# Output rows as 12 products of 128 rows in one accumulator bank, one score task moved among them, and early VectorE work moved to GpSimd and ScalarE

## The chip, the cores and the metric

The kernel runs on one core of a Trainium2 chip. The metric is the time of one execution on the device, in microseconds (us); lower is better. Engines: TensorE does matmuls (PE in the profile, PEld for its weight loads), VectorE (DVE) and ScalarE (ACT) work on tiles element by element and are the two that empty the accumulators (PSUM banks), GpSimd (POOL) works on tiles in SBUF, and SyncE (SP) issues most DMAs. Each engine takes its instructions strictly in program order, so an instruction that waits holds everything behind it on its engine.

## The reference

Two attentions over the same input of 2048 rows and 512 columns, 32 heads of 16 columns each, mixed row by row by a gate:

```python
x = A_x
g = _sigmoid((x * gate_w).sum(-1, keepdims=True))
a = _A_ref(x, A_wq, A_wk, A_wv, A_wo, A_beta)   # 4 segments of 512 rows
b = _B_ref(x, B_wqkv, B_wo)                     # all 2048 rows
return g * a + (1 - g) * b
```

A does causal softmax attention inside each segment of 512 rows, and adds a linear-attention memory that is carried from segment to segment:

```python
logits = jnp.einsum("bhqd,bhkd->bhqk", qs, ks) * scale + mask
a_dot = jnp.einsum("bhqk,bhkd->bhqd", _softmax(logits), vs)
o = g * a_mem + (1.0 - g) * a_dot
```

B is full softmax attention over the 2048 rows. Each ends in a product with its own 512 x 512 output matrix (`A_wo`, `B_wo`). All data is float32.

## The kernel before

**Units.** A prologue (to about 330 us) makes q, k, v and the memory part and stores them in DRAM. The main loop `for k in range(32)` does two units in each iteration: unit `ub = 32 + k` of B (four heads, 512 query rows against 2048 keys) and unit `ua = k` of A (four heads, one segment). There are 8 quads of heads times 4 chunks of 512 rows for either.

**Groups.** An iteration has 37 groups `n` (`NG`); `it = n // 2`. Groups 0 to 31 belong to B, 32 to 36 to A ("the A groups"). `t_group` (L620) does one: two score matmuls (L635, 64 rows each, on the two halves of the array) into two of the three banks `TB[0]`, `TB[1]`, `MB` (`T3`, taken by the longest unused first), then two exponentials on ScalarE (L641); in A groups GpSimd masks the diagonal blocks (L644, "the masks"). `pv` (L647) multiplies the exponentials with the values into the bank `PVB`, two groups behind, at most half a block at a time. Group 1 of an iteration has no `pv`, because group 0 ends the previous A unit and `fin_copy` empties `PVB`.

**Score tasks.** The softmax subtracts the maximum of each row, which is found one iteration ahead: a score task `s_b` (L565) computes 128 queries against 512 keys for two pairs of heads (L572) into one of two double banks `SBK`, used in turn by `rot("s", SBK)`, and VectorE takes the maximum (L574). The 32 tasks of unit 33 + k are laid out by hand, in `plan`: 12 in groups 20 to 31 of iteration k - 1 and 20 in groups 0 to 19 of iteration k, one in each, between the two score matmuls of the group (`between`). Six tasks `s_a` for A go into the A groups.

**Chain of maxima.** At `it == 10`, in group 21, `m_chain(k + 1)` (L578) reduces the maxima (L583) and splits them in a high and a low part: on GpSimd (L592 to L595) for chains 8 to 31, on VectorE (L597 to L599) otherwise. `m_rows` (L601) in group 24 turns the result by a matmul with the identity (L605) and writes it into the q tiles by DMA.

**End of a unit.** `fin_copy(u)` (L660) copies `PVB` to SBUF: for A units up to 30 on VectorE (L664), otherwise on ScalarE (L666). Then `fin_load` reads it back in two layouts, `fin_rec` (L678) takes the reciprocal of the sums on VectorE and multiplies it by the gates (on VectorE while `early` holds, otherwise on GpSimd), `fin_bc` spreads it by DMA into `d`, and `fin_norm` (L699, GpSimd) multiplies, in every second iteration at `it` 9 for B and 13 for A. `beside(k, it)` places these.

**Output matrices.** `load_wo(g)` (L709) at `it == 9` of iterations 1 to 4 reads 128 rows of both output matrices and splits each in a high and a low part on GpSimd (L713, L714), right behind the DMAs in program order.

**Output rows.** The first 1536 output rows are made during iterations 9 to 31, 128 rows in two iterations. `out_split` (L719) splits the operands at the end of an even iteration; then `extras` puts one job at group 1 of each iteration: `a = 0` (A's matrix) in odd iterations k, `a = 1` (B's) in the even ones that follow ("even" and "odd rows" in the text below go by the number n = k - 9 of the job, so a = 0 is an even one). A job is 12 products, three for each of four column groups (`TERMS`: high x high, high x low, low x high). In iterations 9 to 30 `out_rows` (L737) does each product as two of 64 rows, on the two halves of the array, into two banks: one of `T3` and one half of an `SBK` double bank. The score task of group 1 goes in behind the third product (`plan.pop((k, at))` with `at` 1), so `t_group` of group 1 has none. In iteration 31 `out_mm` (L723) does 12 products of 128 rows into one bank.

**Queues.** The program order of each engine is the order of these calls. The tail behind iteration 31 (L1160 on) makes the last 512 rows.

Of the kernel before, what the change touches and what calls it, by code (L numbers as in the profile page):

```python
# [7 lines left out]
FT = mybir.dt.float32  # L8
# [4 lines left out]
AF = mybir.ActivationFunctionType  # L13
OP = mybir.AluOpType
# [7 lines left out]
DM = 512  # L22
# [11 lines left out]
S_LAST = 10  # L34
# [5 lines left out]
def gated_mix_kernel(ctx, tc, xt, wq, wk, wv, wo, beta, wqkv, wob, gate_w, out):  # L40
    nc = tc.nc
    outr = out.rearrange("b s d -> (b s) d")
# [63 lines left out]
    SBK = [PS.tile([128, 2, C], FT, name=f"sbk{i}") for i in range(2)]  # L106
# [9 lines left out]
    def misc():  # L116
        return bank(mode["misc"])
# [12 lines left out]
    def rot(key, lst):  # L130
        i = cnt.get(key, 0)
        cnt[key] = i + 1
        return lst[i % len(lst)]
# [162 lines left out]
    TERMS = ((0, 0), (0, 1), (1, 0))  # L296
# [281 lines left out]
    def m_chain(k):  # L578
        mx = pair_max(k)
        if k == 1:  # L580
            nc.vector.memset(mx[:, 0], 0.0)
        if k < 32:
            nc.vector.tensor_reduce(mx[:, 1], MXB.pop(32 + k).rearrange("q j p i c -> q (j p) i c"), axis=AX.X,  # L583
                                    op=OP.max)
        else:
            nc.vector.memset(mx[:, 1], 0.0)
        del MX[k]
        mx = mx.rearrange("q u h i -> q (u h i)")
        m8 = M8[k] = W.tile([128, 2, 32], FT, name="m8")
        hi = W.tile([128, 32], HF, name="mhi")  # L590
        if 8 <= k < 32:
            nc.gpsimd.tensor_scalar(mx, mx, -1.0 / AUX, None, op0=OP.mult)  # L592
            nc.gpsimd.tensor_copy(hi, mx)
            nc.gpsimd.tensor_copy(m8[:, 0], hi)
            nc.gpsimd.tensor_tensor(m8[:, 1], mx, hi, op=OP.subtract)  # L595
        else:
            nc.vector.tensor_scalar(hi, mx, -1.0 / AUX, None, op0=OP.mult)  # L597
            nc.vector.tensor_copy(m8[:, 0], hi)
            nc.vector.scalar_tensor_tensor(m8[:, 1], mx, -1.0 / AUX, hi, op0=OP.mult, op1=OP.subtract)  # L599
# [16 lines left out]
    AT = {}  # L616
# [30 lines left out]
    def pv(u, it, lo=0, hi=None):  # L647

        kd, qd, c = UN[u]
        g, q = divmod(qd, 2)  # L650
        q0 = 128 * it if kd == "A" else 0
        hi = hi or C - q0
        last = 2 if kd == "A" else NT - 1
        vt = VA[(u // 2) % 2] if kd == "A" else VB[g % 2]
        for h in range(4):
            pt = PT[u, it, h]
            nc.tensor.matmul(PVB[32 * h:32 * h + E + 1, q0 + lo:q0 + hi], vt[:, it, 4 * q + h, :], pt[:, lo:hi],  # L657
                             start=it == 0 and lo == 0, stop=it == last and q0 + hi == C, skip_group_check=True)

    def fin_copy(u):  # L660

        ps = W.tile([128, C], FT, name="pvs", bufs=1)
        if u < 31:
            nc.vector.tensor_copy(ps, PVB)  # L664
        else:
            nc.scalar.activation(ps, PVB, AF.Copy)  # L666
        AT["pd", u] = D.tile([4, 32, C], FT, name=f"pd{u}")
        nc.sync.dma_start(AT["pd", u].rearrange("h r t -> (h r) t"), ps)
# [9 lines left out]
    def fin_rec(u):  # L678
        kd, qd, c = UN[u]
        r = AT.pop(("r", u))  # L680
        nc.vector.reciprocal(r, r)  # L681
        early = u % 32 < 7 or u in (31, 63)
        if kd == "A" and not early:
            nc.gpsimd.tensor_scalar(r, r, nq[:, qd:qd + 1], None, op0=OP.mult)
            nc.gpsimd.tensor_tensor(r, r, grow[:, 0, c], op=OP.mult)
        elif kd == "A":
            nc.vector.scalar_tensor_tensor(r, r, nq[:, qd:qd + 1], grow[:, 0, c], op0=OP.mult, op1=OP.mult)
        else:
            (nc.vector if early else nc.gpsimd).tensor_tensor(r, r, grow[:, 1, c], op=OP.mult)  # L689
        AT["rd", u] = D.tile([128, E], FT, name=f"rd{u}")  # L690
        nc.sync.dma_start(AT["rd", u], r)
# [16 lines left out]

    def load_wo(g):  # L709
        for a, w in enumerate((wo, wob)):  # L710
            raw = AT["o"][1][:, g, a]
            nc.sync.dma_start(raw, w[g * 128:(g + 1) * 128, :])
            nc.gpsimd.tensor_copy(AT["wh"][:, g, a], raw)  # L713
            nc.gpsimd.tensor_tensor(AT["wl"][:, g, a], raw, AT["wh"][:, g, a], op=OP.subtract)  # L714

# [4 lines left out]
        nc.scalar.activation(AT["oh"], o_cols(c, t), AF.Copy)  # L720
        nc.gpsimd.tensor_tensor(AT["ol"], o_cols(c, t), AT["oh"], op=OP.subtract)

    def out_mm(c, t, a):  # L723

        b = misc()
        for n, (oi, wi, g) in enumerate([(oi, wi, g) for oi, wi in TERMS for g in range(4)]):
            nc.tensor.matmul(b, (AT["oh"], AT["ol"])[oi][:, g, a], (AT["wh"], AT["wl"])[wi][:, g, a],
                             start=n == 0, stop=n == 11)
        if a == 0:
            AT["yo"] = AT["L"].tile([128, DM], FT, name="yo")  # L730
            nc.scalar.activation(AT["yo"], b, AF.Copy)
        else:
            tt = 4 * c + t
            nc.vector.tensor_tensor(AT["yo"], b, AT["yo"], op=OP.add)
            nc.sync.dma_start(outr[tt * 128:(tt + 1) * 128, :], AT["yo"])

    def out_rows(c, t, a, inner):  # L737
        b = [misc(), rot("s", SBK)[:, 0]]
        for n, (oi, wi, g) in enumerate([(oi, wi, g) for oi, wi in TERMS for g in range(4)]):
            for j in range(2):  # L740
                r = slice(64 * j, 64 * j + 64)
                nc.tensor.matmul(b[j], (AT["oh"], AT["ol"])[oi][r, g, a], (AT["wh"], AT["wl"])[wi][r, g, a],  # L742
                                 start=n == 0, stop=n == 11)
            if n == 2:
                for f in inner:
                    f()
                rot("s", SBK)
        if a == 0:
            AT["y"] = [AT["L"].tile([128, DM], FT, name=n) for n in ("yo", "yp")]
            nc.scalar.activation(AT["y"][0], b[0], AF.Copy)  # L750
            nc.vector.tensor_copy(AT["y"][1], b[1])
        else:
            tt = 4 * c + t
            y0, y1 = AT["y"]
            y2 = AT["L"].tile([128, DM], FT, name="yq")
            nc.scalar.activation(y2, b[0], AF.Copy)
            nc.vector.tensor_tensor(y1, b[1], y1, op=OP.add)
            nc.gpsimd.tensor_tensor(y0, y0, y2, op=OP.add)
            nc.gpsimd.tensor_tensor(y0, y0, y1, op=OP.add)
            nc.sync.dma_start(outr[tt * 128:(tt + 1) * 128, :], y0)  # L760

    def tail_ops(t):
        s = XT[t // 2][:, t % 2]
# [30 lines left out]
    def todo(fn, *a):  # L794
        return lambda: fn(*a)
# [33 lines left out]
    for tt in range(NT):  # L829
        c, tl = divmod(tt, 4)  # L830
# [230 lines left out]
    def extras(k):  # L1061

        pre, post = {}, {}
        if not k:
            for n in range(4):
                pre[2 * n] = [fill[n - 4]]
        post[2 * S_LAST + 4] = [todo(m_rows, k + 1)]
        for n, at in [(k - 9, 1)] + [(23, 2 * OMI)] * (k == 31):
            if n >= 0:
                rows = (n // 8, n // 2 % 4, n % 2)  # L1070
                pre[at] = [todo(out_rows, *rows, plan.pop((k, at))) if k < 31 else todo(out_mm, *rows)]
        return pre, post

    def beside(k, it):
# [33 lines left out]
    plan = {}  # L1108
# [15 lines left out]
    for k in range(32):  # L1124
        ua, ub = k, 32 + k
        banks = T3 + [b[:, 0] for b in SBK] * (k == 31)
        for n in range(NG):
            it = n // 2 if n < NG - 1 else NT + 2
            mid = plan.pop((k, n)) if n < 2 * NT and (k, n) in plan else []
            t_group(*(ub, n) if n < 2 * NT else (ua, n - 2 * NT), banks, mid)  # L1130
            for f in plan.get((k, n), []) + ex[k][0].get(n, []):
                f()
            pvs(k, n)
            for f in ex[k][1].get(n, []):
                f()
            if n % 2 == 0 and n < NG - 1:
                continue
            beside(k, it)
            if it == S_LAST:
                m_chain(k + 1)  # L1140
            if it == 4 and not k:
                late()
            if it == 4 and not k:
                load_q(ub + 2)
                for c in range(NC4):
                    load_kb(2, c)
            if it == NT and k < 29:
                load_q(ub + 3)
                load_kb(k + 3)
            if it == 6 and k < 31:  # L1150
                load_q(ua + 1)
                load_ka(ua + 1)
                if (ua + 1) % 2 == 0:
                    load_va(ua + 1)
            if it == 9:
                if k % 2 == 0 and k < 30:
                    load_vb(k // 2 + 1)
                if 1 <= k <= 4:
                    load_wo(k - 1)
    pv(31, 2)  # L1160
    fin_copy(31)
    fin_bc(63)
# [52 lines left out]
```

## Time and profile before

| | us |
|---|---|
| median of 3 runs | 1825.24 (1824.66 to 1825.6) |
| the profiled execution | 1825.88 |
| its span, first to last instruction | 1824.2 |
| TensorE clock granted in it | 0.996 of full speed |

The profile is of one execution. Its page gives busy time by engine, the span in 40 slices, the chain of work that ended last, and groups of instructions. A timeline lists instructions in order of time: start, duration, engine, line, operation, output <- inputs (partitions x elements, type), count; neighbours of one kind are merged, and the brackets hold the idle time ahead of it and what ended it. "PE" durations of matmuls overlap, so the time that a matmul costs is read from one start to the next. Times in a timeline are counted from the span's start.

### The profile page before, as it was taken

The page shows a single profiled execution, that of the slowest core. Times are in us where ns is not written, and L with a number is a line of the kernel's source. Part 1 is how long each engine was busy: PE and PEld are TensorE (multiplying, and loading weights), DVE is VectorE, ACT ScalarE, POOL GpSimd, SP SyncE. Part 2 cuts the span into 40 slices and gives each one's busy share as a digit, 9 for nine tenths or more (in the row PEclk, how much of TensorE's full clock was granted, in tenths as well). Part 3 has the DMA queues.
Part 4 walks back from the last instruction along what each step waited for, and adds up shares of the span by engine and source line. Part 5 has one row for each costly group of instructions (what it writes and reads, how often), then busy time and mean ns, then how long its engine had stood idle before and what let it go on. Part 6 is the DMA issues. An engine that isn't in the chain of part 4 may idle for free.

```text
span 1824.2 us, 44323 instructions
## 1 busy us (share of the span) xinstructions
PE 1786.8 (98%) x17781; PEld 645.1 (35%) x17781; DVE 1590.9 (87%) x1787; ACT 1459.3 (80%) x2741; POOL 339.5 (19%) x691
## 2 busy tenths in 40 slices
PE   8999999999999999999999999999999999999998
PEld 6554445222222222333333333333333333333325
DVE  7745786699999999999999999999999999999932
ACT  4454444588989999989898989898989898989894
POOL 4400000001212111112121222122212221222122
PEclk9999999999999999999999999999999999999999
DMA  5654534322323232223232323232323232323111
GB/s 196 152 153 134 159 104 115 75 81 73 93 74 93 64 85 70 77 65 88 65 87 67 86 70 82 71 88 69 85 69 86 68 86 68 86 66 87 46 38 62
DMA packets 162482, 158.92 MB, mean 87 GB/s; under 512 B 40140, under 2 KB 126620, under 8 KB 162276
## 3 DMA queue, kind: packets, MB, share of 16 engines
q1 hardware_dynamic: 158692, 149.29, 29.5%
q0 software_dynamic: 3296, 6.27, 1.8%
q8 instruction: 140, 2.29, 0.5%
q14 instruction: 66, 0.54, 0.1%
q10 hardware_dynamic: 288, 0.52, 0.1%
HBM read 103.38 MB, written 50.86 MB: 85 GB/s over the span
## 4 chain that ended last, share of the span: by engine, by line
PE 78%; DVE 14%; ACT 4%; issue 2%; DMA 1%; POOL 0%; SPq 0%; ACTq 0%; DVEq 0%; POOLq 0%
PE pvb L657 28%; DVE mxb L574 12%; PE tb L635 12%; PE sbk L572 9%; PE mb L635 6%; PE tb L332 3%; ACT raw L641 3%; PE tb L742 2%; PE mb L332 2%; PE sbk L550 2%; PE tb L302 2%; PE sbk L302 2%; PE pvb L332 2%; PE mb L742 1%; PE sbk L332 1%
## 5 line engine op out<-in xcount | busy, mean ns | idle before, releaser
L574 DVE TENSOR_REDUCE mxb<-sbk 128x2 f32<-128x1024 f32 x1024 | 1172.5, 1212 | 21.7 <-PE sbk L572 11.1
L641 ACT ACTIVATE raw<-tb 128x512 f32<-128x512 f32 x1555 | 884.0, 600 | 61.1 <-PE tb L635 25.1
L657 PE MATMUL pvb<-raw,vb 128*17 128x256 f32 (+1 forms) x8072 | 644.4, 388 | 0.0
L572 PE MATMUL sbk<-kb,qb 64*128 64x512 f16 x2048 | 552.7, 378 | 8.4 <-DVE mxb L574 7.3
L641 ACT ACTIVATE raw<-mb 128x512 f32<-128x512 f32 x782 | 469.1, 600 | 33.7 <-PE mb L635 16.7
L635 PE MATMUL tb<-qb,kb 64*128 64x512 f16 x1342 | 467.9, 380 | 2.4 <-ACT raw L641 1.3
L635 PEld LDWEIGHTS <-kb 64*128 64x128 f16 x2048 | 143.5, 93 | 414.1 <-issue 408.8
L657 PEld LDWEIGHTS pvb<-raw,vb 128*17 128x17 f32 x8072 | 137.8, 95 | 402.9 <-issue 393.5
L635 PE MATMUL mb<-qb,kb 64*128 64x512 f16 x679 | 258.4, 381 | 0.0
L644 POOL TENSOR_SCALAR_AFFINE_SELECT raw<-raw 128x256 f32<-128x256 f32 (+1 forms) x320 | 115.4, 361 | 324.4 <-ACT raw L641 316.0
L572 PEld LDWEIGHTS <-qb 64*128 64x128 f16 x2048 | 137.4, 93 | 44.3 <-issue 33.7
L558 DVE TENSOR_REDUCE mx<-sbk 128x2 f32<-128x1024 f32 (+1 forms) x128 | 133.9, 1088 | 6.9 <-PE sbk L554 5.7
L657 PE MATMUL pvb<-raw,va 128*17 128x256 f32 (+2 forms) x1280 | 103.2, 383 | 3.7 <-ACT pvs L666 0.9
L701 POOL TENSOR_TENSOR o<-o,d 128x512 f32<-128x512 f32 x31 | 39.5, 1273 | 217.6 <-DMA d<-rd 156.6
L560 DVE TENSOR_REDUCE mx<-sbk 128x4 f32<-128x512 f32 x64 | 60.6, 947 | 12.5 <-PE sbk L554 12.5
L550 PE MATMUL sbk<-ka,qa 64*128 64x512 f16 (+3 forms) x512 | 70.7, 296 | 0.0
L635 PE MATMUL tb<-qa,ka 64*128 64x512 f16 (+3 forms) x339 | 61.8, 302 | 0.0
L347 DVE SCALAR_TENSOR_TENSOR phi<-phe,phi 128x512 f32<-128x512 f32 x24 | 16.6, 692 | 51.6 <-ACT phe L346 51.6
L689 POOL TENSOR_TENSOR rec<-rec,grow 128x16 f32<-128x16 f32 x24 | 5.3, 222 | 275.8 <-DVE rec L681 275.8
L554 PE MATMUL sbk<-cmask,crows 64*128 64x64 bf16 x1024 | 52.7, 189 | 0.0
L332 PEld LDWEIGHTS <-ws 128*128 128x128 f16 x384 | 37.1, 98 | 43.5 <-issue 2.9
L554 PEld LDWEIGHTS <-crows 64*128 64x128 bf16 x1024 | 46.4, 94 | 13.9
(358 smaller groups left out, 1621.8 us busy)
## 6 DMA issues: line engine op xcount, KB each, us to landing
vb<-vdB SPq DMA_DIRECT2D x16, 1088.0 KB
pd<-pvs SPq DMA_DIRECT2D x64, 256.0 KB
kb<-dB SPq DMA_DIRECT2D x60, 256.0 KB
dB<-st SPq DMA_DIRECT2D x64, 128.0 KB
dA<-st SPq DMA_DIRECT2D x64, 128.0 KB
o<-pd SPq DMA_DIRECT2D x64, 128.0 KB
d<-rd SPq DMA_DIRECT2D x63, 128.0 KB
kb<-dB SPq DMA_DIRECT2D x60, 128.0 KB
```

The source lines that it names most:

```text
L302: nc.tensor.matmul(b, x[:, n % 4, tl * 128:(tl + 1) * 128], (WVA if kd == "A" else WV)[wi][:, n % 4, :], start=n == 0, stop=n == 11)
L332: nc.tensor.matmul(b, WS[ws][w][wi][:, k, :], (XH, XL)[xi][c][:, k, :], start=n == 0, stop=n == 11)
L550: nc.tensor.matmul(b[:, j, c0:c0 + n], q_of(u)[r, p, i * 128:(i + 1) * 128], k_of(u, p)[r, :n], start=True, stop=False)
L554: nc.tensor.matmul(b[:, j, c0 + n - 128 + w.start:c0 + n - 128 + w.stop], crows[r, n2 - 1], cmask[r, n2 - 1, w], start=False, stop=n2 == 2)
L558: nc.vector.tensor_reduce(m[:, :, p, i], b[:, :, :n], axis=AX.X, op=OP.max)
L560: nc.vector.tensor_reduce(m[:, :, :, i], b.rearrange("q j (p k) -> q j p k", p=2)[:, :, :, :n], axis=AX.X, op=OP.max)
L572: nc.tensor.matmul(b[:, j], q_of(u)[r, p, i * 128:(i + 1) * 128], k_of(u, p)[r, kc * C:(kc + 1) * C], start=True, stop=True)
L574: nc.vector.tensor_reduce(MXB[u][:, :, p, i, kc], b, axis=AX.X, op=OP.max)
L635: nc.tensor.matmul(bs[j][:, c0:c0 + w], k_of(u, h // 2)[r, 128 * it:128 * it + 128], q_of(u)[r, h // 2, q0:], start=True, stop=True)
L641: nc.scalar.activation(pt, bs[j], AF.Exp, scale=AT["esc", kd, qd // 2])
L644: nc.gpsimd.affine_select(out=m, in_=m, pattern=[[1, 128]] if n < 2 else [[0, 2], [1, 128]], compare_op=OP.is_ge, fill=0.0, base=0, channe ...
L657: nc.tensor.matmul(PVB[32 * h:32 * h + E + 1, q0 + lo:q0 + hi], vt[:, it, 4 * q + h, :], pt[:, lo:hi], start=it == 0 and lo == 0, stop=it ...
```

## The change

Five edits:

1. `out_rows` goes; `out_mm` does all jobs: 12 products of 128 rows into one bank of `T3`. A job with a = 0 ends in one ScalarE copy, one with a = 1 in one VectorE add from the bank and the store.
2. The score task among the products is no longer that of group 1 but the last of the unit, that of group 19 (`plan.pop((k, 2 * S_LAST - 1))`), behind the sixth product. Group 1 keeps its own task in `t_group`; group 19 has none.
3. `m_chain` uses GpSimd from chain 2 on (8 before); `fin_rec` counts as early for units 0 and 32 (and 31 and 63) alone, where it was units 0 to 6 and 32 to 38.
4. `fin_copy` of A units 0 to 7 is done by ScalarE.
5. `load_wo` issues the DMAs alone; the four GpSimd operations stand in `split_wo`, called at `it == 14` of the same iteration, behind `beside`.

```diff
@@ m_chain
-        if 8 <= k < 32:
+        if 2 <= k < 32:
@@ fin_copy
-        if u < 31:
+        if 8 <= u < 31:
@@ fin_rec
-        early = u % 32 < 7 or u in (31, 63)
+        early = u % 32 < 1 or u in (31, 63)
@@ load_wo
         for a, w in enumerate((wo, wob)):
+            nc.sync.dma_start(AT["o"][1][:, g, a], w[g * 128:(g + 1) * 128, :])
+
+    def split_wo(g):
+        for a in range(2):
             raw = AT["o"][1][:, g, a]
-            nc.sync.dma_start(raw, w[g * 128:(g + 1) * 128, :])
             nc.gpsimd.tensor_copy(AT["wh"][:, g, a], raw)
             nc.gpsimd.tensor_tensor(AT["wl"][:, g, a], raw, AT["wh"][:, g, a], op=OP.subtract)
@@ out_mm
-    def out_mm(c, t, a):
+    def out_mm(c, t, a, inner=()):
 
         b = misc()
         for n, (oi, wi, g) in enumerate([(oi, wi, g) for oi, wi in TERMS for g in range(4)]):
             nc.tensor.matmul(b, (AT["oh"], AT["ol"])[oi][:, g, a], (AT["wh"], AT["wl"])[wi][:, g, a],
                              start=n == 0, stop=n == 11)
+            if n == 5:
+                for f in inner:
+                    f()
@@ out_rows
-    def out_rows(c, t, a, inner):
-        b = [misc(), rot("s", SBK)[:, 0]]
...
@@ extras
-                pre[at] = [todo(out_rows, *rows, plan.pop((k, at))) if k < 31 else todo(out_mm, *rows)]
+                pre[at] = [todo(out_mm, *rows, plan.pop((k, 2 * S_LAST - 1)) if k < 31 else ())]
@@ main loop
                 if 1 <= k <= 4:
                     load_wo(k - 1)
+            if it == 14 and 1 <= k <= 4:
+                split_wo(k - 1)
```

More of the change, by code (lines that the diff above doesn't have):

```diff
@@ L735, in out_mm @@
             nc.sync.dma_start(outr[tt * 128:(tt + 1) * 128, :], AT["yo"])
-    def out_rows(c, t, a, inner):
-        b = [misc(), rot("s", SBK)[:, 0]]
[L739 to L760, printed above, removed]
     def tail_ops(t):
```

## The prediction

> **What bounds the kernel now.** I read the page first: busy shares, then the chain of waits.
>
> ```profile
> PE 1786.8 (98%) x17781; PEld 645.1 (35%) x17781; DVE 1590.9 (87%) x1787; ACT 1459.3 (80%) x2741; POOL 339.5 (19%) x691
> ...
> PE 78%; DVE 14%; ACT 4%; issue 2%; DMA 1%; POOL 0%; SPq 0%; ACTq 0%; DVEq 0%; POOLq 0%
> ```
>
> TensorE and VectorE are both nearly full, so shares don't say which of them sets the pace. The order of time does. First the VectorE timeline of iteration 8, which has no output rows (start, duration, engine, line, count, idle before).
>
> ```profile
> 687.36 0.21 DVE L583 TENSOR_REDUCE mx<-mxb 128x16 f32<-128x64 f32 x1
> ...
> 705.34 1.23 DVE L574 TENSOR_REDUCE mxb<-sbk 128x2 f32<-128x1024 f32 x1 [0.35 <-PE tb L635]
> 706.48 0.68 DVE L664 COPY pvs<-pvb 128x512 f32<-128x512 f32 x1
> 707.07 12.53 DVE L574 TENSOR_REDUCE mxb<-sbk 128x2 f32<-128x1024 f32 x11
> ...
> 731.03 0.20 DVE L583 TENSOR_REDUCE mx<-mxb 128x16 f32<-128x64 f32 x1
> 731.15 2.35 DVE L574 TENSOR_REDUCE mxb<-sbk 128x2 f32<-128x1024 f32 x2
> ```
>
> Eleven maxima, each some 1.23 long and overlapping the next a little, are one block of 12.53: (12.53 - 1.23) / 10 = 1.13 us each, without a gap. The idle 0.35 ahead of 705.34 comes once an iteration, behind the A groups. Now TensorE in iteration 9, which has output rows.
>
> ```profile
> 748.36 0.39 PE L635 MATMUL mb<-qb,kb 64*128 64x512 f16 x1
> ...
> 749.50 0.37 PE L635 MATMUL mb<-qb,kb 64*128 64x512 f16 x1
> 749.99 0.50 PE L742 MATMUL tb<-wh,oh 64*128 64x512 f32 x1
> ...
> 750.79 0.39 PE L572 MATMUL sbk<-kb,qb 64*128 64x512 f16 x2
> ...
> 753.11 0.60 PE L572 MATMUL sbk<-kb,qb 64*128 64x512 f16 x2
> 753.34 0.38 PE L635 MATMUL mb<-qb,kb 64*128 64x512 f16 x1
> ...
> 754.20 0.39 PE L635 MATMUL tb<-qb,kb 64*128 64x512 f16 x1
> ```
>
> Group 2 starts at 753.11 and group 3 at 754.20: where it waits for nothing, TensorE does a group in 1.09, and VectorE needs 1.13 for the group's maximum. So groups with one score task each go at **VectorE's pace**, TensorE being held by the two score banks. The output rows (749.99 to 753.11) are the exception: TensorE sets the time there, and VectorE starves.
>
> ```profile
> 749.00 1.23 DVE L574 TENSOR_REDUCE mxb<-sbk 128x2 f32<-128x1024 f32 x1 [0.35 <-PE tb L635]
> 750.14 0.68 DVE L664 COPY pvs<-pvb 128x512 f32<-128x512 f32 x1
> 751.23 1.23 DVE L574 TENSOR_REDUCE mxb<-sbk 128x2 f32<-128x1024 f32 x1 [0.41 <-PE sbk L572]
> 753.33 0.69 DVE L751 COPY yp<-sbk 128x512 f32<-128x512 f32 x1 [0.88 <-PE sbk L742]
> 753.94 11.39 DVE L574 TENSOR_REDUCE mxb<-sbk 128x2 f32<-128x1024 f32 x10
> ...
> 776.76 0.20 DVE L583 TENSOR_REDUCE mx<-mxb 128x16 f32<-128x64 f32 x1
> ...
> 794.73 1.23 DVE L574 TENSOR_REDUCE mxb<-sbk 128x2 f32<-128x1024 f32 x1 [0.35 <-PE tb L635]
> ...
> 799.59 11.40 DVE L574 TENSOR_REDUCE mxb<-sbk 128x2 f32<-128x1024 f32 x10
> ```
>
> From one L583 (the chain of maxima) to the next is 43.67 without output rows (687.36 to 731.03) and 45.73 with them (731.03 to 776.76).
>
> **Early chains and gates.** Up to iteration 7, VectorE does the tail of m_chain and the gate's products.
>
> ```profile
> 416.50 0.21 DVE L583 TENSOR_REDUCE mx<-mxb 128x16 f32<-128x64 f32 x1
> 416.74 0.91 DVE L597 TENSOR_SCALAR mhi<-mx 128x32 f16<-128x32 f32 x1
> ...
> 462.39 0.21 DVE L583 TENSOR_REDUCE mx<-mxb 128x16 f32<-128x64 f32 x1
> ...
> 463.05 8.00 DVE L574 TENSOR_REDUCE mxb<-sbk 128x2 f32<-128x1024 f32 x7
> ```
>
> A chain keeps VectorE 0.66 (462.39 to 463.05), against 0.12 where GpSimd does the tail (731.03 to 731.15). At 416.74, beside load_wo's split, one small operation alone took 0.91. After the change, chains 2 to 7, and the gates from iteration 2 on, stand as in iteration 8, which has both on GpSimd already. The six stretches from chain 2 (416.50) to chain 8 (687.36) take 270.9; six of 43.67 take 262.0: **8.9** gained. GpSimd, 19% busy, hides what it takes over; without that cover the gain would be gone, since the rows that wait for it are VectorE's old wait over again.
>
> **fin_copy on ScalarE**, for u = 0 to 7, one in each of iterations 1 to 8. VectorE is relieved of 707.07 - 706.48 = 0.59. What is late next is ScalarE, which has exponentials in a row there:
>
> ```profile
> 705.61 1.26 ACT L641 ACTIVATE raw<-tb 128x512 f32<-128x512 f32 x2
> 706.77 0.59 ACT L641 ACTIVATE raw<-mb 128x512 f32<-128x512 f32 x1
> ```
>
> The second of the pair starts at 705.61 + 1.26 - 0.60 = 706.27, the next 0.50 later. A copy of that length goes in at 706.11 and pushes the exponentials behind it by 0.34. Group 2's second score waits for the bank they free, its values slip 0.3, and group 3 some 0.15. VectorE, earlier by 0.59, is then ready just as group 3's scores are. Bounds: 0 (the slip eats it) and 0.59; I take 0.55, because VectorE is without a gap for 24 us behind it: 8 x 0.55 = **4.4**.
>
> **split_wo at it 14.** The DMAs stay at it 9, at the same place of SyncE's queue. The four GpSimd operations go behind the chain's tail, so m_rows doesn't wait for them. In iterations 2 and 4 they also stand behind fin_norm("A") of it 13, which waits for a DMA, and ahead of the A masks. GpSimd's timeline in iteration 2, then TensorE's:
>
> ```profile
> 463.85 0.61 POOL L713 CAST wh<-o 128x512 fp32r<-128x512 f32 x1 [6.91 <-DMA o<-in_A_wo_dram]
> ...
> 466.45 1.27 POOL L714 TENSOR_TENSOR wl<-o,wh 128x512 fp32r<-128x512 f32 x1
> 472.04 1.27 POOL L701 TENSOR_TENSOR o<-o,d 128x512 f32<-128x512 f32 x1 [4.33 <-DMA d<-rd]
> ...
> 476.34 0.29 POOL L644 TENSOR_SCALAR_AFFINE_SELECT raw<-raw 128x128 f32<-128x128 f32 x1 [0.20 <-ACT raw L641]
> ```
> ```profile
> 476.91 0.62 PE L657 MATMUL pvb<-raw,va 128*17 128x256 f32 x8
> ```
>
> A split lasts 466.45 + 1.27 - 463.85 = 3.87. Behind L701 it ends at 472.04 + 1.27 + 3.87 = 477.18. Four masks of 0.29 follow, to about 478.4, and the A values, which started 0.28 after the end of the fourth mask, start at 478.6 instead of 476.91: 1.7. The same in iteration 4: **-3.4** (bounds 0 and two whole splits, -7.7). Iterations 1 and 3 have no fin_norm; their splits end long before the masks. Early part: 8.9 + 4.4 - 3.4 = 9.9.
>
> **Output rows, iterations 9 to 30.** Each job loses 12 pairs of 64-row products; on even rows (a = 0) also VectorE's copy L751, on odd rows ScalarE's copy L756 and two GpSimd adds. It gets 12 products of 128 rows. The trace has such a job, L727 in iteration 31:
>
> ```profile
> 1754.98 0.39 PE L635 MATMUL tb<-qb,kb 64*128 64x512 f16 x2
> 1755.30 1.20 PE L727 MATMUL mb<-wh,oh 128*128 128x512 f32 x4
> 1756.33 1.07 PE L727 MATMUL mb<-wl,oh 128*128 128x512 f32 x4
> 1757.24 1.07 PE L727 MATMUL mb<-wh,ol 128*128 128x512 f32 x4
> 1758.24 0.39 PE L635 MATMUL sbk<-qb,kb 64*128 64x512 f16 x2
> ```
>
> Four steps from 1756.33 to 1757.24 are 0.228 each. The last four take 1.00, so the step out to 64-row work is 0.32, 0.09 more; the first four take 1.03, 0.12 more. In all 2.94. With the inner task in the middle the job leaves and enters twice: 2.94 + 0.09 + 0.32 (scores to the next product, as 1754.98 to 1755.30) + 0.12 = 3.47. The old job, inner task included, took 753.11 - 749.99 = 3.12. So a 128-row product costs what a 64-row pair does, and **TensorE loses 0.35** a job. The first entry costs nothing: it lies in the wait from 749.50 to 749.99.
>
> For VectorE, group 1 now has its own task beside the inner one. Let S be the start of group 0 (748.36). First maximum S+0.64, pvs copy S+1.78, second maximum S+2.37; six products from S+1.63 bring the inner scores at S+3.21 and, 0.44 later (as 750.79 to 751.23), the inner maximum at S+3.65; group 2 at S+5.10. On even rows the next maximum is 0.64 behind group 2: S+5.74, against 753.94 - 748.36 = S+5.58 now. On odd rows the add starts at about S+5.24 and the maximum 0.61 on, at S+5.85, against 799.59 - 794.73 + 0.64 = S+5.50 now. So groups 2 to 18 come 0.16 or 0.35 later, but one maximum more is done.
>
> That one is missing in group 19. One row more is needed, of m_rows in group 24 of another iteration:
>
> ```profile
> 916.22 0.39 PE L605 MATMUL mb<-ident,m 128*32 128x128 f32 x4
> ```
>
> Without score matmuls between its two halves it goes from 1.13 to 1.09 - 0.23 = 0.86 (753.11 to 753.34 is what they take). VectorE then has lag to spare, and groups 20 to 31 go at TensorE's pace. The gain is 0.27 in group 19, 12 x 0.04 = 0.48 behind it and the chain's 0.12, less m_rows, 0.39, which VectorE's pace hides now and which then stands in the open: 0.48 in all. Net 0.32 on even and 0.13 on odd rows: 11 x 0.45 = **5.0**. Bounds: -0.25 an iteration (the hole brings nothing) and +0.75 (no loss in the job), -5.5 and +16.5.
>
> SyncE's wait for GpSimd's adds goes; nothing on the path waits for it. Iteration 31 and the tail stay.
>
> **Sum.** 9.9 + 5.0 = 14.9. The profiled run took 1825.88 (span 1824.2, 1.7 around it): 1811.0. The median of the runs shown is 0.6 lower: **1810**.
>
> **Rivals.** (1) *The hole brings nothing*: ScalarE fills it. For it: two exponentials at 0.50 need 1.0, more than group 19's 0.86, and group 20's values wait for them. Against: three banks, and slack in each group of 1.13. 9.9 - 5.5 = 4.4: 1821. (2) *VectorE alone decides*: what TensorE loses in the job falls into waits for banks. For it: 0.49 of such a wait ahead of the job now. 9.9 + 16.5 = 26.4: 1799. (3) *GpSimd doesn't keep up*: gates and chains stand behind fin_norm's DMA, the early part brings nothing, nor the rows: 1825. Against: from iteration 8 on this order costs nothing. (4) **Slower: each change of tile size empties the array.** Place: the three exposed changes of an output job. Price: a whole matmul in flight, 0.39 to 0.50, in place of 0.09, so 0.4 more each; 22 x 1.2 = 26.4: 1825.2 - 14.9 + 26.4 = 1837. It decides from 14.9 / 66 = 0.23 more a change. Against it stand the two steps of 0.32 around L727, which are all that the trace has of it in this loop.
>
> The Trainium skill, "TensorEngine Tiling (Array Packing)", Key Properties, holds the rule that speaks against this change: going from one tiling mode to another drains the TensorE. It names no price. By a full drain the time would be rival 4's; the steps of 0.32 beside 0.228 agree that there is a price, and say it is small.
>
> **How the numbers follow.** Forecast 0.50 (1805 to 1815), rival 1 0.20 (1815 to 1821), rival 2 0.18 (1797 to 1805), rivals 3 and 4 0.06 each. From 1800 to 1821 leaves out some 2 in 10: half of rival 2, and 3 and 4. A difference under 0.2% (3.7 us) can't be told from no change: faster 0.88, within 0.06, slower 0.06.
>
> **What would show it.** From chain to chain 43.1 without rows, 45.4 to 45.6 with them; a job of 3.4 to 3.5; no maximum in group 19 and steps of 1.09 behind it; TensorE waiting for masks in iterations 2 and 4. Wrong if the steps around the inner task are far from 0.32, or if groups 20 to 31 stay at 1.13.

## The result, and the profile after

| | before | after |
|---|---|---|
| median, us (5 runs each) | 1825.32 (1824.66 to 1828.94) | 1814.92 (1814.08 to 1815.35) |
| the profiled execution, us | 1825.88 | 1815.07 |
| its span, us | 1824.2 | 1813.3 |
| granted TensorE clock | 0.996 | 0.997 |

After to before is 0.9936, with a 95% interval of 0.9922 to 0.995: some 10.4 us faster. The forecast was 1810, with a range from 1800 to 1821; the time lies in it, and the gain is some seven tenths of the 14.9 forecast.

The two lines of the page that stood first in the prediction, now of the kernel after (busy time by engine; shares of the chain that ended last):

```profile
PE 1778.1 (98%) x17517; PEld 629.4 (35%) x17517; DVE 1577.6 (87%) x1738; ACT 1449.0 (80%) x2738; POOL 323.0 (18%) x711
...
PE 90%; DVE 4%; ACT 2%; DMA 2%; issue 1%; SPq 1%; POOL 0%; ACTq 0%; DVEq 0%; POOLq 0%
```

The busy shares have hardly moved. The chain has: VectorE's part fell from 14% to 4%, and TensorE's rose from 78% to 90%. More groups now go at TensorE's pace.

Where the time went is seen from the starts of the chain of maxima (L583). "Stretch n" is the time from chain n to chain n + 1; it holds the output job of iteration n. Sums of stretches, in us, of the profiled executions:

| stretches | before | after | gained |
|---|---|---|---|
| 1 to 8, no output rows | 359.43 | 350.70 | 8.73 |
| 9 to 29, with output rows | 960.33 | 958.61 | 1.72 |
| chain 30 to the end | 132.80 | 133.21 | -0.41 |

That is 10.0 together, beside 10.4 between the medians. The early edits brought nearly all of it; the output rows, whose 264 products were rewritten, brought 1.3. Stretch 0 took 69.0 before and 68.0 after, but 69.0 to 69.8 in all nine experiments below; it differs from execution to execution and is not counted as a gain.

VectorE's timeline of the kernel after, with an even job (iteration 13, group 0 of TensorE at S = 921.51) and an odd one (iteration 16, S = 1058.40):

```profile
923.89 2.50 DVE L574 TENSOR_REDUCE mxb<-sbk 128x2 f32<-128x1024 f32 x2
927.29 11.41 DVE L574 TENSOR_REDUCE mxb<-sbk 128x2 f32<-128x1024 f32 x10 [0.90 <-PE tb L635]
...
1060.78 2.52 DVE L574 TENSOR_REDUCE mxb<-sbk 128x2 f32<-128x1024 f32 x2
1063.65 0.69 DVE L740 TENSOR_TENSOR yo<-tb,yo 128x512 f32<-128x512 f32 x1 [0.35 <-PE tb L730]
1064.25 11.40 DVE L574 TENSOR_REDUCE mxb<-sbk 128x2 f32<-128x1024 f32 x10
```

The second maximum is now followed at once by the inner one (x2). The maximum of group 2, from which VectorE runs without a gap again, starts at S+5.78 on the even row and at S+5.85 on the odd one (before: S+5.58 and S+5.50). So VectorE is later behind the job, as forecast, and one maximum further on.

TensorE's timeline of the kernel after, the odd job:

```profile
1060.03 1.21 PE L730 MATMUL tb<-wh,oh 128*128 128x512 f32 x4
1061.08 0.62 PE L730 MATMUL tb<-wl,oh 128*128 128x512 f32 x2
1061.64 0.39 PE L572 MATMUL sbk<-kb,qb 64*128 64x512 f16 x2
1061.96 0.73 PE L730 MATMUL tb<-wl,oh 128*128 128x512 f32 x2
1062.53 1.08 PE L730 MATMUL tb<-wh,ol 128*128 128x512 f32 x4
1063.54 0.39 PE L635 MATMUL mb<-qb,kb 64*128 64x512 f16 x1
```

The job lasts 1063.54 - 1060.03 = 3.51 with the inner task's pair of scores at 1061.64 in the middle, against 3.12 before.

What the missing task of group 19 brings is read some 20 us later. First TensorE before, in the same iteration 16: groups 18, 20 and 24, the matmul of m_rows, groups 25 and 26, and 32, the first of the A groups:

```profile
1091.22 0.39 PE L635 MATMUL tb<-qb,kb 64*128 64x512 f16 x1
...
1093.48 0.39 PE L635 MATMUL mb<-qb,kb 64*128 64x512 f16 x1
...
1098.01 0.39 PE L635 MATMUL tb<-qb,kb 64*128 64x512 f16 x1
...
1099.15 0.39 PE L605 MATMUL tb<-ident,m 128*32 128x128 f32 x4
1099.47 0.39 PE L635 MATMUL tb<-qb,kb 64*128 64x512 f16 x1
...
1100.57 0.39 PE L635 MATMUL tb<-qb,kb 64*128 64x512 f16 x1
...
1107.18 0.39 PE L635 MATMUL tb<-qa,ka 64*128 64x512 f16 x2
```

And after, groups 18, 19, 20 (its second row is its values), 21, 22, 24, 25 and 32:

```profile
1081.51 0.39 PE L635 MATMUL tb<-qb,kb 64*128 64x512 f16 x1
...
1082.64 0.39 PE L635 MATMUL tb<-qb,kb 64*128 64x512 f16 x2
...
1083.52 0.39 PE L635 MATMUL mb<-qb,kb 64*128 64x512 f16 x1
...
1084.08 0.80 PE L657 MATMUL pvb<-raw,vb 128*17 128x256 f32 x8
1084.81 0.39 PE L635 MATMUL tb<-qb,kb 64*128 64x512 f16 x1
...
1085.90 0.39 PE L635 MATMUL tb<-qb,kb 64*128 64x512 f16 x1
...
1088.09 0.39 PE L635 MATMUL tb<-qb,kb 64*128 64x512 f16 x1
...
1089.39 0.39 PE L635 MATMUL tb<-qb,kb 64*128 64x512 f16 x1
...
1097.07 0.42 PE L635 MATMUL tb<-qa,ka 64*128 64x512 f16 x2
```

Before, steps of 1.13 (VectorE's pace) run up to group 24; that group, with m_rows in it, takes 1099.47 - 1098.01 = 1.46, and behind it TensorE catches up at 1.10. After, group 19 takes 1083.52 - 1082.64 = 0.88, the step behind it 1084.81 - 1083.52 = 1.29, and from there on a group takes 1.09 to 1.10 and the one with m_rows 1.30. From group 18 to the A groups that makes 1107.18 - 1091.22 = 15.96 before and 1097.07 - 1081.51 = 15.56 after: the empty group brings **0.40**, and the job takes 0.20 or 0.35 of it away again. Typical stretches agree: even rows 45.80 before and 45.59 after, odd rows 45.65 and 45.64.

### The profile page after: what moved, and what is told of

It is laid out like the page before. It is cut to its first block, busy times and chain, and to the rows that moved or that the text cites. A ratio compares the mean times of both kernels' runs of the same rounds, so it can differ in the third digit from the quotient of the medians.

```text
span 1813.3 us, 43733 instructions
## 1 busy us (share of the span) xinstructions
PE 1778.1 (98%) x17517; PEld 629.4 (35%) x17517; DVE 1577.6 (87%) x1738; ACT 1449.0 (80%) x2738; POOL 323.0 (18%) x711
## 4 chain that ended last, share of the span: by engine, by line
PE 90%; DVE 4%; ACT 2%; DMA 2%; issue 1%; SPq 1%; POOL 0%; ACTq 0%; DVEq 0%; POOLq 0%
PE pvb L657 35%; PE tb L635 14%; PE sbk L572 12%; PE mb L635 7%; PE tb L730 3%; PE tb L332 3%; DVE mxb L574 3%; PE sbk L550 2%; PE mb L332 2%; PE tb L302 2%; PE sbk L302 2%; PE pvb L332 1%; PE mb L730 1%; ACT raw L641 1%; PE sbk L332 1%; PE sbk L554 1%
## 5 line engine op out<-in xcount | busy, mean ns | idle before, releaser
L572 PE MATMUL sbk<-kb,qb 64*128 64x512 f16 x2048 | 572.8, 379 | 4.5 <-DVE mxb L574 4.3
L635 PEld LDWEIGHTS <-kb 64*128 64x128 f16 x2048 | 129.0, 93 | 416.6 <-issue 411.9
L644 POOL TENSOR_SCALAR_AFFINE_SELECT raw<-raw 128x256 f32<-128x256 f32 (+1 forms) x320 | 115.6, 364 | 283.8 <-ACT raw L641 276.0
L572 PEld LDWEIGHTS <-qb 64*128 64x128 f16 x2048 | 122.5, 93 | 32.8 <-issue 23.2
L701 POOL TENSOR_TENSOR o<-o,d 128x512 f32<-128x512 f32 x31 | 39.5, 1275 | 170.5 <-DMA d<-rd 158.0
```

The source lines that it names most:

```text
L572: nc.tensor.matmul(b[:, j], q_of(u)[r, p, i * 128:(i + 1) * 128], k_of(u, p)[r, kc * C:(kc + 1) * C], start=True, stop=True)
L635: nc.tensor.matmul(bs[j][:, c0:c0 + w], k_of(u, h // 2)[r, 128 * it:128 * it + 128], q_of(u)[r, h // 2, q0:], start=True, stop=True)
L644: nc.gpsimd.affine_select(out=m, in_=m, pattern=[[1, 128]] if n < 2 else [[0, 2], [1, 128]], compare_op=OP.is_ge, fill=0.0, base=0, channe ...
```

## The experiments

The theory: VectorE's lag behind the job and behind the early copies sets the end; the early part (edits 3 to 5) is worth some 9, the rows 1 to 2, because the inner task costs in the job nearly what the empty group returns. Rivals: the rows gain in the job and lose in a wait elsewhere; TensorE's drains cost the rows; GpSimd is late in the early part. All nine kernels compute the whole output. "Before" in each is the kernel before on the same chip. They were timed in three lots, each with runs of the kernel before of its own: early_only, rows_only, split_11 and hole_18 (median of before 1824.81); no_inner, inner_last, copy_dve and best_noinner (1825.03); and pairs_noinner (1824.78).

### The two halves of the change, one at a time

early_only is the kernel before with edits 3, 4 and 5 alone (chains, gates, copies, splits); rows_only is it with edits 1 and 2 alone. In terms of the kernel after, shortened (rows_only has the splits back in `load_wo`, early_only has the old `out_rows` again, both as in the listing of before):

```diff
rows_only
-        if 2 <= k < 32:
+        if 8 <= k < 32:
...
-        if 8 <= u < 31:
+        if u < 31:
...
-        early = u % 32 < 1 or u in (31, 63)
+        early = u % 32 < 7 or u in (31, 63)
...
-            if it == 14 and 1 <= k <= 4:
-                split_wo(k - 1)
early_only
-                pre[at] = [todo(out_mm, *rows, plan.pop((k, 2 * S_LAST - 1)) if k < 31 else ())]
+                pre[at] = [todo(out_rows, *rows, plan.pop((k, at))) if k < 31 else todo(out_mm, *rows)]
```

> The kernel before with edits 3, 4 and 5 alone (chains and gates on GpSimd, fin_copy on ScalarE, split_wo at it 14). Theory (the early part carries nearly all of the gain): stretches 1 to 8 as in the changed kernel, 350.7 us against 359.4, and the stretches with output rows as before (45.80 and 45.65): 8.7 faster, about 1816.6. Rival (the rows carry the forecast 5.0, the early part only about 5): about 1820.

> The kernel before with edits 1 and 2 alone (12 products of 128 rows, the last score task among them). Theory: stretches 9 to 29 lose 1.8 us in all, the end gives 0.4 back: 1.4 faster, about 1824, within what can be told from no change. Rival (the forecast of 5.0 holds and the trace hides it): about 1820.

Measured: early_only 1815.56, ratio 0.9948 (0.9935 to 0.9962); rows_only 1823.66, ratio 0.9993 (0.9984 to 1.0002). The early part is worth 9.2. The rows alone, 1.2, can't be told from no change. The stretches put each where it was expected: 1 to 8 took 350.53 in early_only and 359.30 in rows_only; 9 to 29 took 960.55 and 958.61. The halves add up to the whole, so neither covers the other.

### The splits ahead of the masks

```diff
split_11
-            if it == 14 and 1 <= k <= 4:
+            if it == 11 and 1 <= k <= 4:
                 split_wo(k - 1)
```

> The changed kernel with split_wo at it 11 instead of it 14, behind the chain's tail but ahead of fin_norm. Theory (in iterations 2 and 4 the split stands ahead of the A masks and holds TensorE 1.6 us each time): stretches 3 and 5 fall from 44.9 to 43.3 and the time by 3.2 to about 1811.7. Rival (those two stretches are long because fin_norm is late, not the split): no change, 1814.9.

Measured: 1811.95, ratio 0.993 (0.9917 to 0.9944). GpSimd's timeline of the kernel after in iteration 2 (rows of splits L716 and L717, fin_norm L701, masks L644):

```profile
467.91 1.28 POOL L701 TENSOR_TENSOR o<-o,d 128x512 f32<-128x512 f32 x1 [7.92 <-DMA d<-rd]
469.12 0.62 POOL L716 CAST wh<-o 128x512 fp32r<-128x512 f32 x1
...
471.73 1.26 POOL L717 TENSOR_TENSOR wl<-o,wh 128x512 fp32r<-128x512 f32 x1
472.95 1.76 POOL L644 TENSOR_SCALAR_AFFINE_SELECT raw<-raw 128x128 f32<-128x128 f32 x6
```

and TensorE's of the same stretch:

```profile
473.29 0.89 PE L657 MATMUL pvb<-raw,va 128*17 128x256 f32 x5 [1.04 <-POOL raw L644]
```

GpSimd waits 7.92 for the DMA that fin_norm needs; the split and six masks stand behind it in a row, and the A values on TensorE wait 1.04 for a mask, with more lost in the steps behind. GpSimd's timeline of split_11 has the split early, and the masks wait for ScalarE alone:

```profile
462.80 0.61 POOL L716 CAST wh<-o 128x512 fp32r<-128x512 f32 x1 [2.44 <-DMA o<-in_A_wo_dram]
...
468.25 1.27 POOL L701 TENSOR_TENSOR o<-o,d 128x512 f32<-128x512 f32 x1 [1.59 <-DMA d<-rd]
470.50 0.29 POOL L644 TENSOR_SCALAR_AFFINE_SELECT raw<-raw 128x128 f32<-128x128 f32 x1 [0.97 <-ACT raw L641]
```

Stretches 3 and 5 took 44.93 and 44.84 in the kernel after, 43.25 both here. The two waits cost **3.27**, where the prediction had 3.4. Stretches 1 to 8 together took 347.25 instead of 350.70, 3.45 less; the other 0.18 is spread over stretches that no split disturbs. The medians lie 2.97 apart.

### The copies back on VectorE

```diff
copy_dve
-        if 8 <= u < 31:
+        if u < 31:
             nc.vector.tensor_copy(pvs, PVB)
```

> The changed kernel with fin_copy of units 0 to 7 back on VectorE. Theory (0.59 less on VectorE, of which group 3's later scores take 0.17): stretches 1 to 8 are 0.42 longer each, 3.4 slower than the changed kernel, about 1818.3. Rival (the slip of the values on TensorE eats the gain): the same 1814.9.

Measured: 1817.94, ratio 0.996 (0.9946 to 0.9973). Undisturbed early stretches take 43.68 with VectorE's copy and 43.25 with ScalarE's. VectorE's timeline of copy_dve, iteration 7:

```profile
612.91 0.68 DVE L664 COPY pvs<-pvb 128x512 f32<-128x512 f32 x1
613.50 12.53 DVE L574 TENSOR_REDUCE mxb<-sbk 128x2 f32<-128x1024 f32 x11
```

and of the kernel after:

```profile
609.67 13.85 DVE L574 TENSOR_REDUCE mxb<-sbk 128x2 f32<-128x1024 f32 x12 [0.35 <-PE tb L635]
```

Without the copy the twelve maxima are one block, but a looser one: from the first to the last start 13.85 - 1.23 = 12.62, that is 11 steps of 1.147 on average; at 1.13 it would be 12.43. One step alone is long, 1.30 to the fourth maximum, that of group 3. So of the 0.59 that the copy took from VectorE, 0.19 went into waits for group 3's late scores, which leaves 0.40; the stretches show 0.43, the eight copies together 353.89 - 350.70 = 3.2, where the two disturbed stretches 3 and 5 are in it.

### The empty group one earlier

The empty group 19 gave less than forecast. In the kernel after, ScalarE's timeline shows the two exponentials of group 19:

```profile
1083.13 1.09 ACT L641 ACTIVATE raw<-tb 128x512 f32<-128x512 f32 x2
```

The code tells what waits: in an even group n, `pv(ub, n // 2 - 1, ...)` takes the block whose second half is the group just before. The values in group 20 start at 1084.08, while group 19's second exponential ends at 1083.13 + 1.09 = 1084.22; those eight products take 0.80 instead of 0.63. Then an odd group behind the hole should not wait:

```diff
hole_18
-                pre[at] = [todo(out_mm, *rows, plan.pop((k, 2 * S_LAST - 1)) if k < 31 else ())]
+                pre[at] = [todo(out_mm, *rows, plan.pop((k, 2 * S_LAST - 2)) if k < 31 else ())]
```

> The changed kernel with the task of group 18 among the products in place of that of group 19, so the group without a task is an even one. Theory (group 20's values wait for the exponentials of group 19, which comes too soon behind group 18; values of an odd group use older exponentials): the step of 1.28 behind the empty group falls to 1.13 or less, 0.17 an iteration, 22 x 0.17 = 3.7 faster than the changed kernel, about 1811. Rival (ScalarE is short of time behind any empty group): the same 1814.9.

Measured: 1813.24, ratio 0.9935 (0.9921 to 0.9948), hardly told from the kernel after. TensorE's timeline of hole_18, groups 18, 19 and 20, and the values of group 18:

```profile
1082.12 0.39 PE L635 MATMUL tb<-qb,kb 64*128 64x512 f16 x1
...
1082.44 0.79 PE L657 MATMUL pvb<-raw,vb 128*17 128x256 f32 x8
1083.16 0.39 PE L635 MATMUL tb<-qb,kb 64*128 64x512 f16 x1
...
1084.26 0.39 PE L635 MATMUL mb<-qb,kb 64*128 64x512 f16 x1
```

The step behind the hole fell from 1.29 to 1.10, as expected. But the empty group itself took 1.04 instead of 0.88: it is an even one, and its own values (0.79) wait for group 17's exponentials. Of the 0.17 an iteration that was expected, 0.07 came (even stretches 45.52, odd 45.57). The wait moved; my expectation had looked at one side of the hole only.

### No inner task, and the inner task last

```diff
no_inner
-                pre[at] = [todo(out_mm, *rows, plan.pop((k, 2 * S_LAST - 1)) if k < 31 else ())]
+                pre[at] = [todo(out_mm, *rows, ())]
inner_last
-            if n == 5:
+            if n == 11:
                 for f in inner:
                     f()
```

In the first, group 19 keeps its task and the products run through. In the second, the inner task comes behind all twelve; TensorE changes tile size only once into the job and once out of it.

> The changed kernel with no score task among the 12 products; every group keeps its own, so none is empty. Theory (the maximum of group 2 sets the time of groups 2 to 18, and the task among the products delays it through two changes of tile size): the job takes 2.95 instead of 3.51, group 2's maximum starts at S+5.25 (even) and S+5.3 (odd) instead of S+5.74 and S+5.85, the gain of the empty group (0.39) is lost; even rows 45.46, odd ones 45.45 against 45.59 and 45.64: 3.5 faster than the changed kernel, about 1811. Rival (the moved task is what the rows gain by, as the forecast had it): 22 x 0.4 = 9 slower, about 1824.

> The changed kernel with the moved score task behind the 12th product instead of the sixth: one way out and in of 128-row work less, so TensorE's job is 0.34 shorter, but the task's maximum starts only at S+5.0 instead of S+3.65. Theory (VectorE decides up to group 18): group 2's maximum goes from S+5.74 to S+6.13 on even rows and, behind the add, from S+5.85 to S+6.74 on odd ones: 11 x 1.3 = 14 slower than the changed kernel, about 1829. Rival (TensorE's job decides): 22 x 0.34 = 7.5 faster, about 1807.

Measured: no_inner 1810.83, ratio 0.9917 (0.9904 to 0.9931); inner_last 1828.9, ratio 1.0019 (1.001 to 1.0028), slower than before. VectorE's timeline of no_inner (even job, S = 921.04):

```profile
926.28 4.62 DVE L574 TENSOR_REDUCE mxb<-sbk 128x2 f32<-128x1024 f32 x4 [1.64 <-PE tb L635]
```

and of inner_last (odd job, S = 971.76):

```profile
976.81 1.23 DVE L574 TENSOR_REDUCE mxb<-sbk 128x2 f32<-128x1024 f32 x1 [1.45 <-PE sbk L572]
977.95 0.68 DVE L740 TENSOR_TENSOR yo<-mb,yo 128x512 f32<-128x512 f32 x1
978.55 4.61 DVE L574 TENSOR_REDUCE mxb<-sbk 128x2 f32<-128x1024 f32 x4
```

In no_inner VectorE idles 1.64 in the even job instead of 0.90, and 1.13 instead of 0.35 in an odd one (S = 1057.41). Yet the kernel is the faster one: group 2's maximum starts at S+5.24 instead of S+5.78, and at S+5.33 instead of S+5.85 in the odd job. So the inner task costs 0.54 in an even job and 0.52 in an odd one, more than the 0.40 that its empty place returns; stretches fall to 45.41 and 45.45. Chain 30 to the end took 132.53 instead of 133.21. In inner_last the maximum of group 2 starts at S+6.79, 0.94 later than in the kernel after, and odd stretches take 46.59, 0.95 more. TensorE's job is shorter there, 3.22 from the first product (973.39) to group 2's first scores (976.61) against 3.51, and the kernel loses 14 us: VectorE's lag behind the job decides, not the time that TensorE spends in it.

### Pairs without an inner task

What is the single bank worth by itself? pairs_noinner is no_inner with the old products of 64 rows into two banks in iterations 9 to 30, and the old copies and adds:

```diff
pairs_noinner
-                pre[at] = [todo(out_mm, *rows, plan.pop((k, 2 * S_LAST - 1)) if k < 31 else ())]
+                pre[at] = [todo(out_rows if k < 31 else out_mm, *rows)]
+    def out_rows(c, t, a):
+        b = [misc(), rot("s", SBK)[:, 0]]
+        for n, (oi, wi, g) in enumerate([(oi, wi, g) for oi, wi in TERMS for g in range(4)]):
+            for j in range(2):
+                r = slice(64 * j, 64 * j + 64)
...
```

> The kernel without a task among the products (as no_inner), but with the old 12 pairs of 64-row products in two banks, one of them half a score bank, and the old copies and adds; the early part as changed. It tells what the one bank of 128-row products is worth apart from where the task stands. Theory (a 128-row product costs TensorE what a pair does, and the worth is in the banks: the pair job starts only when group 0's maximum has left its score bank, at S+1.9 instead of S+1.6, and VectorE has a copy more on even rows): group 2's maximum at S+5.56 against S+5.25 and S+5.3, 22 x 0.28 = 6 slower than no_inner, about 1817. Rival (the shape and the banks don't matter, only that no task stands among the products): 1811, as no_inner.

Measured: 1816.52, ratio 0.9953 (0.9939 to 0.9967). Even and odd stretches of 45.81 and 45.75 are some 0.35 above no_inner's, which is 5.7 between the medians. TensorE's timeline of pairs_noinner, first and last pair of an even job with S = 920.90:

```profile
922.52 0.49 PE L748 MATMUL tb<-wh,oh 64*128 64x512 f32 x1
922.82 0.49 PE L748 MATMUL sbk<-wh,oh 64*128 64x512 f32 x1
...
925.24 0.39 PE L748 MATMUL tb<-wh,ol 64*128 64x512 f32 x1
925.47 0.39 PE L748 MATMUL sbk<-wh,ol 64*128 64x512 f32 x1
```

and VectorE's:

```profile
921.54 1.23 DVE L574 TENSOR_REDUCE mxb<-sbk 128x2 f32<-128x1024 f32 x1 [0.35 <-PE tb L635]
...
925.96 0.69 DVE L753 COPY yp<-sbk 128x512 f32<-128x512 f32 x1 [1.47 <-PE mb L635]
926.57 4.61 DVE L574 TENSOR_REDUCE mxb<-sbk 128x2 f32<-128x1024 f32 x4
```

The products into `sbk` start 0.30 behind their partners, because group 0's maximum holds that bank until 921.54 + 1.23 = 922.77, and they are still 0.23 behind at the last column group. VectorE's copy of that bank stands ahead of group 2's maximum: S+5.67 against no_inner's S+5.24. I had put the start of the whole job behind that bank, at S+1.9; the half in `tb` starts at S+1.62, and only the other waits.

### The two that helped, together

best_noinner is the kernel after with the edits of split_11 and no_inner.

> split_wo at it 11 and no score task among the products, both in one. Theory (the two are in different stretches and add up): 1814.9 - 3.0 - 3.5, about 1808.5. Rival (one of them hides the other): 1811 to 1812.

Measured: 1807.54 (1807.12 to 1808.46), ratio 0.9902 (0.9887 to 0.9918): 17.5 us faster than before and some 7 faster than the kernel after. Its stretches are those of the two parents (347.26, 954.66, and 132.73 to the end).

## Why the prediction was right, and too large

| term of the sum, us | forecast | measured | from |
|---|---|---|---|
| chains and gates on GpSimd | 8.9 | 9.0 | 359.43 - 347.25 less the copies' 3.2 |
| eight copies on ScalarE | 4.4 | 3.2 | stretches 1 to 8, copy_dve less after |
| splits behind fin_norm | -3.4 | -3.45 (3.27 of it in stretches 3 and 5) | stretches 1 to 8, after less split_11 |
| output rows | 5.0 | 1.3 | stretches from 9 on, before less after |
| sum | 14.9 | 10.0 | |

**The bound** was read rightly. VectorE's lag decides (inner_last), groups without it go at 1.09, and the chain of waits moved from VectorE to TensorE.

**Chains and gates**: right. copy_dve, which has this edit but not the copies, shows 43.68 a stretch; the 43.67 of iteration 8 had been taken for it. GpSimd had the room, so rival 3 fell. One part of the 9.0 is not told apart: before, the tails of chains 2 and 4 kept VectorE 1.72 and 1.32, beside the splits on GpSimd, and those of chains 3 and 5 to 7 kept it 0.65 or 0.66. These 1.7 us go by moving the chains and perhaps also by moving the splits alone (edit 5); no run has one without the other.

**The copies**: the mechanism held, the size did not. "I take 0.55" was chosen close to the upper bound of 0.59, with the reason that VectorE is without a gap for 24 us behind the copy. It is not quite: the slip of group 3's scores, which the prediction had at 0.15, cost VectorE 0.19, and 0.40 to 0.43 was left. VectorE is freed just when TensorE is late.

**The splits**: right, mechanism and size; one line of the change, `it == 14`, cost 3.27.

**The job on TensorE**: right within 0.04. 3.51 against the 3.47 worked out, group 2's maximum at S+5.78 and S+5.85 against S+5.74 and S+5.85.

**The empty group** is the step that failed, by its size: "0.48 in all", where the trace shows 0.40. Its parts were further off than the sum. The forecast had group 20 at 1.09; it takes 1.29, because its values wait for group 19's exponentials. It had 0.04 for each of twelve groups behind; before, the groups behind m_rows already ran at 1.09 or 1.10, so there was less to gain. And it had m_rows as a new cost of 0.39; before, that group took 1.46, and after, 1.30, so m_rows became cheaper by 0.16. Against a net of 0.32 and 0.13 an iteration stood 0.21 and 0.01: over 11 even and 10 odd jobs 1.2 + 1.2 less. Of the 0.11 to 0.12 a job, 0.08 is the empty group's (read in iteration 16 alone), and on even rows 0.04 the job's. A small difference of large terms was multiplied by 22.

Two things more were missing in the rows' 5.0. Iteration 30 was counted like the others, but groups 20 to 31 have no task there, so TensorE sets their pace anyway: the job's loss stays and nothing comes back. From the first A group of iteration 29 to that of iteration 30 TensorE took 44.75 before and 45.14 after. With the 0.13 counted as gain, the 0.41 lost is 0.5 off. And stretches 24 and 29 were 0.30 and 0.25 longer than their like, stretch 11 by 0.2: 0.7 together. Other runs with 128-row jobs show such stretches too, some at other places (16, 18 and 28 in rows_only and copy_dve, by 0.22 to 0.28), the three profiles with pairs (before, early_only, pairs_noinner) none. In the traces each begins with one late exponential on ScalarE (last section); why that one is late stays open.

**Rivals.** The first (ScalarE fills the hole) was half true: the wait that it named exists, at 0.2 an iteration, but the hole still brings 0.40. The second (VectorE alone decides) fell: what TensorE loses in the job comes out as a later maximum. The fourth, that each change of tile size empties the array at 0.4 or more, fell: in the job after, the step from the scores to the next product is 1061.96 - 1061.64 = 0.32 and four products with the step out take 1063.54 - 1062.53 = 1.01, that is 0.32 for the last beside 0.228 for the others. The Trainium skill, "TensorEngine Tiling (Array Packing)", Key Properties, says that a change of tiling mode drains the engine; the trace agrees that it costs something, and puts it at about 0.09 a change. inner_last, with fewer changes, was the slower kernel.

That the forecast lay in the range all the same comes from the early part, which held two thirds of the gain that was expected and whose terms had rows of their own in the trace of before, and from the width of the range: its slow end, 1821, allowed for rows that lose 5.5. No errors cancelled; the rows and the copies, 3.7 and 1.2 too large, were off the same way.

## What to carry to other kernels

Judge an edit by when the engine that sets the pace can start the first item behind the disturbed place, and not by what any engine does inside it: against the kernel after, no_inner lets VectorE idle longer in the job and is faster, inner_last shortens TensorE's job and is slower. A task moved into the one place where another engine sets the pace is not free there (0.54 or 0.52 here), and the gap that it leaves is refilled by the next engine in line (0.40 came back). An engine that looks idle, like GpSimd at 18%, still delays others by its order: put an operation that nobody waits for ahead of the one that waits for a DMA, not behind it.

## What the runs showed of the hardware that was not expected

A product of 128 rows and 512 columns costs a step of 0.228 (the prediction's rows 1756.33 and 1757.24), and a pair of 64-row products on the two halves of the array 0.24 to 0.25 on average, the slower first step included (pairs_noinner: eleven steps from 922.52 to 925.24 in `tb`, and from 922.82 to 925.47 in `sbk`). So halving the rows and doubling the products changes TensorE's time by little. When one half of the array starts late, it stays late: 0.30 at the first pair, 0.23 at the twelfth.

The waits behind the splits differ between profiled executions of the same order of work: stretches 3 and 5 took 44.42 to 45.16 in the six profiles with the splits at `it == 14` and the copies on ScalarE (after, early_only, hole_18, no_inner, inner_last, pairs_noinner). They follow the start of fin_norm, which waits for its DMA: it started 8.78 to 9.51 behind the chain, and in all twelve stretches 35.62 to 35.66 remained from there to the next chain. With the splits at `it == 11` fin_norm started at 8.79 to 9.24, and the stretches took 43.25 whatever it did.

The stretches that are longer than their like go back to ScalarE. In stretches 11, 24 and 29 of the kernel after, one exponential (at 852.77, 1416.05 and 1642.27) starts 0.33 or 0.34 behind the end of the wait ahead of it, 0.27 or 0.28 later than its like in a stretch of normal length, and what follows it is late. Counted in the trace with the waits, these are the 1600th, 2880th and 3392nd instructions of ScalarE. In stretches 16, 18 and 28 of rows_only they are the 2112th, 2240th and 3264th, in copy_dve the same; all are multiples of 64. So the places belong to the program: they move when an edit, such as the copies of edit 4, changes the number of ScalarE's instructions. What ScalarE does there, the trace does not show.
